# One 512-column stream per weight load in the late down products of a two-mixture kernel

## The chip, the core and the metric

The program runs on one core of one Trainium2 chip, alone. Its time is device time in microseconds, the median of several executions of one program. Three executions of the kernel before took 929.62, 928.58 and 929.4 us; the median is 929.4.

## The reference, cut to what matters

The reference is a kernelized attention whose output goes through two dense mixtures, one after the other. The change touches only the last product of each, `... @ w_out`, called the down product here.

```
x = attention(q, k, v, omega)                 # 2304 tokens x 512
g = x @ w_gate; val = x @ w_val               # 512 -> 1536
x = (g * sigmoid(g) * val) @ w_out            # 1536 -> 512, first down product
h = x @ w_in                                  # 512 -> 2048
g = where(h >= 1, h, where(h <= -1, 0, (h + 1)**2 / 4))
out = g @ w_out                               # 2048 -> 512, second down product
```

## The kernel before

**Three matmuls for one product.** Every 32-bit factor is kept as two tiles of the type fp32r, a high part and a low rest. `split3` (L418 to L420) multiplies them with three matmuls: high by high, high by low, low by high. Each matmul loads a stationary block of 128 by 128 into TensorE (LDWEIGHTS, shown as PEld) and streams the moving operand through it.

**Stages.** Attention and the first mixture's early steps share the time up to about 225 us. The rest of the first mixture and all of the second form the late part: four passes, two for each mixture, over five blocks of tokens (four of 512 tokens, the last of 256). In a pass `late_up` makes the up products of each block: seven products of 256 columns built from sums and differences of quarters (`set_up`), so that one product is saved. ScalarE (ACT) and VectorE (DVE) turn them into activations and split these into rows `hl` or `hlr` (`row_out`). `late_down` then multiplies each row by its part of `w_out` and adds it up in four banks of PSUM, `acc[0]` to `acc[3]`, a whole pass long.

**The down products.** In the first mixture (`down1`) the stationary block is a 128-column piece of the weight and the tokens stream. In the second (`down2`, and `down_end` for the last two rows) the stationary block is a 128-token piece of the row and the weight's 512 columns stream. In a name such as `bank<-hl,w` the moving tile comes first: `bank<-hl,w` is a product of the first mixture, `bank<-w,hl` one of the second. Both stream 256 columns at a time and go over the same stationary blocks twice, once for each half of the bank.

**What orders the work.** No engine order is written out by hand. `Planner` simulates the engines with a cost for each operation and records an instruction when its simulated engine comes to it. PE takes the operation of the lowest rank first: up products have 2.0, down products 2.1, so a down product is placed when its row is ready by the plan and no up product is. DVE and ACT go by rank too: the preparation of the weights (`stage`: from the two words of a 64-bit number to 32 bits, lines L435 to L442, stored in DRAM as `w32`) comes last at 1.5, and `w_feed` fetches the weights of the next pass back as soon as slots are free. `copy` (L399 on ACT, L401 on DVE) goes to whichever of the two would be done sooner by the plan. PE's cost is `c_pe`. On the chip each engine runs its list in order and waits on semaphores.

Of the kernel before, what the change touches and what calls it, by code (L numbers as in the profile page):

```python
# [28 lines left out]
P = 128  # L29
TB = 256  # L30
# [255 lines left out]


def c_pe(n):
    return max(0.109, n * 0.1134 / 256)


@with_exitstack
def performer_moe_kernel(ctx: ExitStack, tc: tile.TileContext, qX, kX, vX, om, ident,
# [17 lines left out]
    acc = []  # L311
# [105 lines left out]
    def split3(ps, l_hi, l_lo, r_hi, r_lo, first, last, shared=False):  # L417
        nc.tensor.matmul(ps, l_hi, r_hi, start=first, stop=False, skip_group_check=shared)  # L418
        nc.tensor.matmul(ps, l_hi, r_lo, start=False, stop=False, skip_group_check=shared)  # L419
        nc.tensor.matmul(ps, l_lo, r_hi, start=False, stop=last, skip_group_check=shared)  # L420
# [570 lines left out]
    def evac_late(a, kb, n):  # L991
        nt = blocks[kb][1]
        rng = (osb, xin)[n % 2]
        xb = yield Get(rng)
        yield x2_part_ready[a, kb, n]
        pb = x2_part.pop((a, kb, n))
        x, part, ac = xb[:, 0:nt], pb[:, 0:nt], acc[n][:, 0:nt]
        if n % 2:
            yield Op("ACT", c_act(nt), lambda: nc.scalar.activation(x, ac, AF.Copy, scale=0.5))
            pl.set(acc_free[n])  # L1000
            yield from two(x, x, part, nt, ALU.add)
        else:
            yield Op("DVE", c_dve(nt), lambda: nc.vector.scalar_tensor_tensor(
                out=x, in0=ac, scalar=0.5, in1=part, op0=ALU.mult, op1=ALU.add))
            pl.set(acc_free[n])
        pl.put(xpart, pb)
        pl.cur.rank = 1.0
        if a < len(SETS1) - 1:
            yield from dma(x2q[a][kb][:, n, 0:nt], x, P * nt * 4)
            pl.set(x2p_ready[a + 1, kb, n])  # L1010
        else:
            yield from dma(x2d[n // 2][:, n % 2, kb * 512:kb * 512 + nt], x, P * nt * 4)
        pl.put(rng, xb)
        if a == len(SETS1) - 1:
            x2_cnt[kb] = x2_cnt.get(kb, 0) + 1
            if x2_cnt[kb] == KD:
                pl.set(x2_ready[kb])
# [24 lines left out]
    def out1(step, h_ev, res):  # L1042
        k, fp = step
        first, last, end = run[step]
        for i in range(2):
            yield wready["o", 2 * fp + i]
        yield h_ev
        ws = [wslot["o", 2 * fp + i] for i in range(2)]
        hl = res[0]
        for n in range(KD):  # L1050
            d, c = divmod(n, 2)
            if first and c == 0:
                acc1[d] = yield Get(bank, -2)
            for i in range(2):
                yield Op("PE", 3 * c_pe(TB), lambda: split3(
                    acc1[d][:, c * TB:(c + 1) * TB], ws[i][:, 0, n * P:(n + 1) * P], ws[i][:, 1, n * P:(n + 1) * P],
                    hl[:, 0, i * TB:(i + 1) * TB], hl[:, 1, i * TB:(i + 1) * TB],
                    first and c == 0 and i == 0, last and i == 1, True), kind="moe")
            if last and c == 1:
                pl.spawn(evac1(k, d, end, acc1[d]))  # L1060
        pl.put(hrow, res[1])
        for f in (2 * fp, 2 * fp + 1):
            if last_use[f] == step:
                wfree(("o", f), wring)

    def moe1():
        pend = None
        for step in steps1:
# [12 lines left out]
            for s in ("g", "v"):  # L1081
                yield wready[s, 2 * fp]
                ps = yield Get(bank, -1)
                for i in range(2):
                    f = 2 * fp + i
                    yield wready[s, f]
                    w = wslot[s, f]
                    yield Op("PE", 12 * c_pe(TB), lambda: gemm(ps[:, i * TB:(i + 1) * TB], w), kind="moe")
                    if last_use[f] == step:
                        wfree((s, f), wring)  # L1090
                if s == "g":
                    pl.spawn(elem1(ps, vps, v_ev, (h_ev, res)))
                else:
                    vps.append(ps)
                    pl.set(v_ev)
# [119 lines left out]
    half2 = [slice(0, 256), slice(256, 512)]  # L1215
    rows = {}
    before = got = None
    for m, a, order, sets in passes:
        for j in order:
            for c in sets:  # L1220
                n = 2 if m == 1 and j < 4 else 1 if m == 1 else 4 if j < 4 else 2
# [213 lines left out]
    def evac2(a, j, c):  # L1435
        t0, nt = blocks[j]
        x = yield Get(osb)
        end = a == len(SETS2) - 1
        ro = out[t0 + c * P:t0 + (c + 1) * P, :] if end else opart[a, j, c]
        if a == 0:  # L1440
            yield from copy(x, acc[c], 512, False)
            pl.set(acc_free[c])
            yield from dma(ro, x, 262144)
        else:
            yield part2_ready[a - 1, j, c]
            pb = part2.pop((a - 1, j, c))
            yield Op("DVE", c_dve(512), lambda: nc.vector.tensor_tensor(out=x, in0=acc[c], in1=pb, op=ALU.add))
            pl.set(acc_free[c])
            pl.put(xpart, pb)
            yield from dma(ro, x, 262144)  # L1450
        if not end:
            pl.set(opart_ready[a, j, c])
        pl.put(osb, x)
# [11 lines left out]
    def down1(a, j, f, hl, cols, first, last):  # L1465

        nt = blocks[j][1]
        yield wready["o", f]
        w = wslot["o", f]
        for n in range(KD):  # L1470
            if first:
                while len(acc) <= n:
                    acc.append((yield Get(bank, -2)))
                yield acc_free[n]
                acc_free[n] = Ev()


            def prod():
                for t in range(0, nt, TB):
                    h = slice(cols.start + t, cols.start + t + TB)  # L1480
                    split3(acc[n][:, t:t + TB], w[:, 0, n * P:(n + 1) * P], w[:, 1, n * P:(n + 1) * P],
                           hl[:, 0, h], hl[:, 1, h], first and t == 0, last, True)
            yield Op("PE", 3 * c_pe(nt), prod)
            if last:
                pl.spawn(evac_late(a, j, n))

    def down2(a, j, f, hl, cols, first, last):
        nt = blocks[j][1]
        yield wready["p", f]
        w = wslot["p", f]  # L1490
        for c in range(nt // P):
            if first:
                yield acc_free[c]
                acc_free[c] = Ev()
            h = slice(cols.start + c * P, cols.start + (c + 1) * P)


            def prod():
                for d in half2:
                    split3(acc[c][:, d], hl[:, 0, h], hl[:, 1, h], w[:, 0, d], w[:, 1, d], first and d.start == 0, last, True)  # L1500
            yield Op("PE", 3 * c_pe(512), prod)
            if last:
                pl.spawn(evac2(a, j, c))

    def evac_end(a, j, c, done):
        t0 = blocks[j][0]
        x = yield Get(osb)
        yield part2_ready[a - 1, j, c]
        pb = part2.pop((a - 1, j, c))
        for h, ev in zip(half2, done):  # L1510
            yield ev
            yield Op("DVE", c_dve(256), lambda: nc.vector.tensor_tensor(out=x[:, h], in0=acc[c][:, h], in1=pb[:, h], op=ALU.add))
            last = pl.spawn(dma(out[t0 + c * P:t0 + (c + 1) * P, h], x[:, h], P * 1024))
        yield last

    def down_end(a, j, pair, hl):
        ws = []
        for f, _ in pair:
            yield wready["p", f]
            ws.append(wslot["p", f])  # L1520
        for c in range(2):
            hs = [slice(cols.start + c * P, cols.start + (c + 1) * P) for _, cols in pair]
            for i in range(2 - c):
                def prod(i=i, c=c):
                    for d in half2:
                        split3(acc[c][:, d], hl[:, 0, hs[i]], hl[:, 1, hs[i]], ws[i][:, 0, d], ws[i][:, 1, d], False, i + c == 1, True)
                yield Op("PE", 3 * c_pe(512), prod)
            if c == 0:
                pl.spawn(evac2(a, j, c))
        done = [Ev(), Ev()]  # L1530
        pl.spawn(evac_end(a, j, 1, done))
        for h, ev in zip(half2, done):
            yield Op("PE", 3 * c_pe(TB), lambda: split3(
                acc[1][:, h], hl[:, 0, hs[1]], hl[:, 1, hs[1]], ws[1][:, 0, h], ws[1][:, 1, h], False, True, True))
            pl.set(ev)
# [140 lines left out]
```

## Time and profile before

| what | value |
|---|---|
| median of the timed runs | 929.4 us |
| the profiled execution's span, first to last instruction | 928.9 us |
| PE, matmuls | 920.5 us, 99%, 9244 instructions |
| PEld, weight loads | 905.8 us, 98%, 9244 instructions |
| DVE | 775.1 us, 83%, 1496 instructions |
| ACT | 511.7 us, 55%, 1131 instructions |
| 16 DMA engines, main queue | 48.5% of their time |

The profile shows one execution. Its own time outside the span isn't shown; the median is 0.5 us above the span. A matmul's recorded duration reaches from its start to its last result, so that durations overlap: what one costs TensorE is the distance from start to start.

### The profile page before, as it was taken

How to read it: one execution, taken by the hardware profiler on the slowest of the kernel's cores; microseconds unless marked ns; L12 is line 12 of the kernel's file. 1: busy time of each engine (PE TensorE's matmuls, PEld its weight loads, DVE VectorE, ACT ScalarE, POOL GpSimd, SP SyncE). 2: the span in 40 equal slices, each digit the busy share in tenths (PEclk: the TensorE clock that was granted, in tenths of full speed). 3: DMA queues.
4: the chain of work that ended last, by engine and by line, in shares of the span. 5: the costliest groups of instructions: out<-in, count | busy, mean ns of one | idle time of the engine just before them, and what ended most of it. 6: DMA issues, size and time to landing. Idle time of an engine off the chain costs nothing.

```text
span 928.9 us, 22669 instructions
## 1 busy us (share of the span) xinstructions
PE 920.5 (99%) x9244; PEld 905.8 (98%) x9244; DVE 775.1 (83%) x1496; ACT 511.7 (55%) x1131; POOL 61.7 (7%) x53
## 2 busy tenths in 40 slices
PE   9999999999999999999999999999999999999998
PEld 7899999999999999999999999999999999999998
DVE  5999888766989998999989999999797669767553
ACT  7888877544445545554545556554555445444331
POOL 0222314222000000000000000000000000000000
PEclk9999999999999999999999999999999999999999
DMA  7578356555665374946476836264313131403022
GB/s 242 193 246 280 111 178 214 191 182 178 221 233 179 114 245 167 303 131 197 142 231 218 271 110 200 80 225 139 126 58 125 47 102 47 137 12 103 9 84 91
DMA packets 88665, 147.71 MB, mean 159 GB/s; under 512 B 8304, under 2 KB 43888, under 8 KB 88560
## 3 DMA queue, kind: packets, MB, share of 16 engines
q1 hardware_dynamic: 88560, 146.26, 48.5%
q8 instruction: 72, 1.18, 0.5%
q14 instruction: 33, 0.27, 0.1%
HBM read 103.24 MB, written 42.99 MB: 157 GB/s over the span
## 4 chain that ended last, share of the span: by engine, by line
PE 88%; DVE 5%; DMA 4%; ACT 1%; issue 1%; SPq 0%; DVEq 0%; ACTq 0%
PE bank L418 26%; PE bank L420 25%; PE bank L419 25%; PE bank L654 5%; PE bank L723 2%; PE bank L836 2%; PE bank L792 2%; PE bank L846 1%; DMA wtr<-w32i 1%; DMA ws<-in_w_dram 1%; DMA ws<-in_wo_dram 1%; DMA x2d<-os 1%; DMA xr<-x2p 1%; DMA xq<-x1d 1%; DMA kl<-in_kX_dram 1%
## 5 line engine op out<-in xcount | busy, mean ns | idle before, releaser
L418 PE MATMUL bank<-x1s,w 128*128 128x256 f32 x492 | 138.2, 281 | 0.5 <-ACT eb L399 0.3
L419 PE MATMUL bank<-x1s,w 128*128 128x256 f32 x492 | 136.4, 277 | 0.0
L420 PE MATMUL bank<-x1s,w 128*128 128x256 f32 x492 | 136.4, 277 | 0.0
L418 PEld LDWEIGHTS bank<-x1s,w 128*128 128x128 f32 x492 | 92.5, 188 | 1.6 <-ACT eb L399 0.5
L419 PEld LDWEIGHTS bank<-x1s,w 128*128 128x128 f32 x492 | 92.5, 188 | 0.0
L420 PEld LDWEIGHTS bank<-x1s,w 128*128 128x128 f32 x492 | 92.5, 188 | 0.0
L399 ACT ACTIVATE x1s<-xq 128x512 fp32r<-128x512 f32 x84 | 52.7, 629 | 59.1 <-PE bank L420 34.7
L418 PE MATMUL bank<-x1s,wb 128*128 128x256 f32 x286 | 78.9, 276 | 0.0
L419 PE MATMUL bank<-x1s,wb 128*128 128x256 f32 x286 | 78.9, 276 | 0.0
L420 PE MATMUL bank<-x1s,wb 128*128 128x256 f32 x286 | 78.9, 276 | 0.0
L418 PE MATMUL bank<-x1s,wx 128*128 128x256 f32 x278 | 77.3, 278 | 0.7 <-ACT eb L399 0.7
L419 PE MATMUL bank<-x1s,wx 128*128 128x256 f32 x278 | 76.8, 276 | 0.0
L420 PE MATMUL bank<-x1s,wx 128*128 128x256 f32 x278 | 76.8, 276 | 0.0
L435 ACT ACTIVATE wt<-ws 128x512 f32<-128x512 f32 x68 | 46.0, 678 | 45.2 <-DMA ws<-in_w_dram 24.4
L399 ACT ACTIVATE eb<-bank 128x512 f32<-128x512 f32 x96 | 56.5, 589 | 25.2 <-PE bank L420 24.7
L411 DVE TENSOR_TENSOR x1s<-xq,x1s 128x512 fp32r<-128x512 f32 x90 | 61.7, 686 | 8.0 <-ACT x1s L399 7.8
L663 DVE TENSOR_REDUCE st<-bank 128x4 f32<-128x512 f32 (+1 forms) x76 | 47.9, 657 | 17.8 <-PE bank L654 17.7
L1248 DVE TENSOR_TENSOR gb<-bank,eb 128x512 f32<-128x512 f32 x64 | 43.9, 686 | 12.9 <-PE bank L420 12.7
L399 ACT ACTIVATE hlr<-hb 128x512 fp32r<-128x512 f32 x54 | 34.0, 630 | 36.1 <-PE bank L419 21.9
L418 PEld LDWEIGHTS bank<-x1s,wb 128*128 128x128 f32 x286 | 53.7, 188 | 0.0
L419 PEld LDWEIGHTS bank<-x1s,wb 128*128 128x128 f32 x286 | 53.7, 188 | 0.0
L420 PEld LDWEIGHTS bank<-x1s,wb 128*128 128x128 f32 x286 | 53.7, 188 | 0.0
(253 smaller groups left out, 3328.6 us busy)
## 6 DMA issues: line engine op xcount, KB each, us to landing
ws<-in_w_dram SPq DMA_DIRECT2D x40, 512.0 KB, 4.9
ws<-in_wo_dram SPq DMA_DIRECT2D x28, 512.0 KB, 5.4
xq<-x1d SPq DMA_DIRECT2D x36, 256.0 KB, 4.5
xq<-x2d SPq DMA_DIRECT2D x36, 256.0 KB, 4.2
qi<-in_qX_dram SPq DMA_DIRECT2D x28, 256.0 KB, 4.0
ki<-in_kX_dram SPq DMA_DIRECT2D x22, 256.0 KB, 4.4
x1d<-os SPq DMA_DIRECT2D x18, 256.0 KB, 4.3
op<-os SPq DMA_DIRECT2D x18, 256.0 KB, 2.7
```

The costliest lines, as they stand in the source:

```text
L399: yield Op("ACT", c_act(n), lambda: nc.scalar.activation(dst, src, AF.Copy, scale=1.0 if scale is None else scale))
L411: yield Op("DVE", c_dve(n), lambda: nc.vector.tensor_tensor(out=dst, in0=a, in1=b, op=op), True)
L418: nc.tensor.matmul(ps, l_hi, r_hi, start=first, stop=False, skip_group_check=shared)
L419: nc.tensor.matmul(ps, l_hi, r_lo, start=False, stop=False, skip_group_check=shared)
L420: nc.tensor.matmul(ps, l_lo, r_hi, start=False, stop=last, skip_group_check=shared)
L435: yield Op("ACT", 0.575, lambda: nc.scalar.activation(t, hw.bitcast(F32), AF.Abs))
L654: nc.tensor.matmul(banks[a][:, u * P:(u + 1) * P], xb[h, l, u * P:(u + 1) * P], r[h], start=first and (last or u == 0), stop=last, skip_gr ...
L663: yield Op("DVE", c_dve(256 * n), lambda: nc.vector.tensor_reduce(out=sv[:, a, units, 3 if by_pe else 0], in_=pv[a], axis=AX.X, op=ALU.max ...
L723: nc.tensor.matmul(kp[h, 2 * pr + a, 0:65], es[:, a, u * P + 64 * m:u * P + 64 * m + 64], v[:, 65 * a:65 * a + 65], start=(li == 0 and a = ...
L792: nc.tensor.transpose(tp[:, (a * 2 + t) * P:(a * 2 + t + 1) * P], es[:, a, u * P:(u + 1) * P], ids)
L836: nc.tensor.matmul(banks[t][rows, 65 * h:65 * h + 65], q_t[:, h // 2, h % 2, t * P + 64 * m:t * P + 64 * m + 64], kvr[tiles[t][m], d][:, h ...
L1248: yield Op("DVE", c_dve(512), lambda: nc.vector.tensor_tensor(out=dst, in0=pq(ps), in1=pq(e), op=ALU.add))
```

## The change

The two halves of each late down product become one: the same three matmuls of `split3`, each on 512 columns. This holds for the four blocks of 512 tokens in the first mixture and for all of the second, except the last two half products of the program. The up products, the early down products (`out1`) and the first mixture's block of 256 tokens stay at 256 columns. The planner's cost of a matmul is changed too: at 256 columns it stays 0.1134 us, at 512 columns it falls from 0.2268 to 0.2168 us, and at 128 columns it rises from 0.109 to 0.1134.

```
 def c_pe(n):
-    return max(0.109, n * 0.1134 / 256)
+    return max(0.1134, n / 2400.0 + 0.0035)
...
             def prod():
-                for t in range(0, nt, TB):
-                    h = slice(cols.start + t, cols.start + t + TB)
-                    split3(acc[n][:, t:t + TB], w[:, 0, n * P:(n + 1) * P], w[:, 1, n * P:(n + 1) * P],
-                           hl[:, 0, h], hl[:, 1, h], first and t == 0, last, True)
+                h = slice(cols.start, cols.start + nt)
+                split3(acc[n][:, 0:nt], w[:, 0, n * P:(n + 1) * P], w[:, 1, n * P:(n + 1) * P],
+                       hl[:, 0, h], hl[:, 1, h], first, last, True)
             yield Op("PE", 3 * c_pe(nt), prod)
...
             def prod():
-                for d in half2:
-                    split3(acc[c][:, d], hl[:, 0, h], hl[:, 1, h], w[:, 0, d], w[:, 1, d], first and d.start == 0, last, True)
+                split3(acc[c], hl[:, 0, h], hl[:, 1, h], w[:, 0], w[:, 1], first, last, True)
             yield Op("PE", 3 * c_pe(512), prod)
...
                 def prod(i=i, c=c):
-                    for d in half2:
-                        split3(acc[c][:, d], hl[:, 0, hs[i]], hl[:, 1, hs[i]], ws[i][:, 0, d], ws[i][:, 1, d], False, i + c == 1, True)
+                    split3(acc[c], hl[:, 0, hs[i]], hl[:, 1, hs[i]], ws[i][:, 0], ws[i][:, 1], False, i + c == 1, True)
                 yield Op("PE", 3 * c_pe(512), prod)
```

In the program 2490 matmuls of 256 columns become 1245 of 512, with 1245 weight loads fewer. On PE, at the first late down product between two up products (`x1s_72` by a weight; `hlr` by the weight `wb_3550` is the down product):

```order
 L419 MATMUL bank_70<-x1s_72,w_111 128x256
 L420 MATMUL bank_70<-x1s_72,w_111 128x256
-L418 MATMUL bank_65<-hlr,wb_3550 128x256
-L419 MATMUL bank_65<-hlr,wb_3550 128x256
-L420 MATMUL bank_65<-hlr,wb_3550 128x256
-L418 MATMUL bank_65<-hlr,wb_3550 128x256
-L419 MATMUL bank_65<-hlr,wb_3550 128x256
-L420 MATMUL bank_65<-hlr,wb_3550 128x256
+L418 MATMUL bank_65<-hlr,wb_3550 128x512
+L419 MATMUL bank_65<-hlr,wb_3550 128x512
+L420 MATMUL bank_65<-hlr,wb_3550 128x512
 L418 MATMUL bank_70<-x1s_72,w_117 128x256
```

Six rows became three, at the same place; the neighbours stay.

Further on in the first mixture, PE's list is ordered anew. Before, a down product (`hl` by `wb_3551`) stands right between two products of the up part:

```order
L418 MATMUL bank_67<-x1s_73,w_113 128x256
L419 MATMUL bank_67<-x1s_73,w_113 128x256
L420 MATMUL bank_67<-x1s_73,w_113 128x256
L418 MATMUL bank_65<-hl,wb_3551 128x256
L419 MATMUL bank_65<-hl,wb_3551 128x256
L420 MATMUL bank_65<-hl,wb_3551 128x256
```

With the change the same up product is followed by further up products:

```order
L418 MATMUL bank_67<-x1s_73,w_113 128x256
L419 MATMUL bank_67<-x1s_73,w_113 128x256
L420 MATMUL bank_67<-x1s_73,w_113 128x256
L418 MATMUL bank_70<-x1s_72,wx_957 128x256
L419 MATMUL bank_70<-x1s_72,wx_957 128x256
L420 MATMUL bank_70<-x1s_72,wx_957 128x256
```

Thirty rows of up products now stand ahead of this down product, where none stood before. The interleaving of up and down products is ordered anew in this way between some 390 and 535 us of the trace before; ahead of it and behind it the two orders agree but for one or two places.

On DVE, in the first mixture's late part (`wt` and `ws` are tiles of the weight preparation, L436 to L442; `os` is an accumulator on its way to DRAM, `eb` the copy of a product's bank):

```order
 L411 TENSOR_TENSOR xq_3540<-xq_3537,xq_3540 128x512
-L411 TENSOR_TENSOR hlr<-hb_100,hlr 128x512
-L436 TENSOR_SCALAR wt_78<-wt_78 128x512
-L438 TENSOR_SCALAR wt_78<-wt_78 128x512
-L440 SCALAR_TENSOR_TENSOR wt_78<-ws_76,wt_78 128x512
-L442 SCALAR_TENSOR_TENSOR wt_78<-ws_76,wt_78 128x512
+L401 COPY eb_3529<-bank_69 128x512
+L436 TENSOR_SCALAR wt_78<-wt_78 128x512
 L1003 SCALAR_TENSOR_TENSOR os_103<-bank_65,xr_3526 128x512
```

A bank's copy moved from ACT to DVE, and three steps of the weight preparation moved back behind the accumulator. Over the program seven copies more are on DVE and seven fewer on ACT: 1500 rows on DVE where there were 1493, 869 on ACT where there were 876. SP issues the same number of transfers, those of the weight preparation later among the others.

## Rows read from the trace of the kernel before

**Rows 1.** The page: busy time of engines; PE's share and granted clock by slices.
```profile
PE 920.5 (99%) x9244; PEld 905.8 (98%) x9244; DVE 775.1 (83%) x1496; ACT 511.7 (55%) x1131; POOL 61.7 (7%) x53
...
PE   9999999999999999999999999999999999999998
...
PEclk9999999999999999999999999999999999999999
```

**Rows 2.** Windows: us; busy us (instructions) of PE, PEld, DVE, ACT, POOL; PEclk; DMA.
```profile
225.00:500.00 275.00, 273.64 (x2400) 272.50 (x2399) 256.50 (x486) 142.58 (x262) 1.29 (x1) 1.00 0.61 200
500.00:720.00 220.00, 220.00 (x1942) 219.95 (x1941) 202.40 (x377) 122.44 (x226) 0.00 (x0) 1.00 0.46 149
720.00:929.00 209.00, 204.62 (x1806) 204.42 (x1804) 135.89 (x235) 82.00 (x146) 0.00 (x0) 1.00 0.22 70
425.00:450.00 25.00, 25.00 (x222) 24.95 (x221) 24.83 (x51) 15.05 (x29) 0.00 (x0) 1.00 0.68 222
525.00:575.00 50.00, 50.00 (x444) 50.00 (x443) 50.00 (x94) 31.47 (x59) 0.00 (x0) 1.00 0.56 178
625.00:675.00 50.00, 50.00 (x443) 50.00 (x442) 42.03 (x76) 25.67 (x46) 0.00 (x0) 1.00 0.42 136
```

**Rows 3.** Timeline of PE, 860 to 880 us: start, duration, instruction.
```profile
859.74 0.28 PE L420 MATMUL bank<-wx,hlr 128*128 128x256 f32 x1
859.86 0.28 PE L418 MATMUL bank<-x1s,wx 128*128 128x256 f32 x1
...
879.92 0.28 PE L418 MATMUL bank<-w,hlr 128*128 128x256 f32 x1
```

**Rows 4.** The chain that ended last, 408 to 475 us and behind: start, us, what.
```profile
408.39 0.13 PE bank L420
...
414.14 5.20 DMA xq<-x1d
...
424.33 0.60 DVE gb L1248
...
474.85 0.50 ACT eb L399
475.39 0.38 PE bank L418
```

**Rows 5.** PE's matmuls on `hl`, by windows: us, busy (instructions), clock, DMA.
```profile
408.00:475.00 67.00, 14.14 (x96) 1.00 0.62 195
475.00:929.00 454.00, 137.00 (x1008) 1.00 0.36 117
625.00:929.00 304.00, 99.68 (x748) 1.00 0.26 85
```

**Rows 6.** The same of the matmuls on `hlr`.
```profile
408.00:475.00 67.00, 16.33 (x113) 1.00 0.62 195
475.00:929.00 454.00, 137.48 (x1008) 1.00 0.36 117
625.00:929.00 304.00, 99.75 (x744) 1.00 0.26 85
```

**Rows 7.** Groups by line: weight loads by shape, copies on DVE; busy us, mean ns.
```profile
L418 PEld LDWEIGHTS bank<-hlr,w 128*128 128x128 f32 x80 | 15.0, 188 | 0.0
...
L723 PEld LDWEIGHTS bank<-vi,ebk 128*64 128x64 f32 x640 | 20.2, 137 | 2.2 <-issue 0.3
...
L792 PEld LDWEIGHTS bank<-ids,ebq 128*128 128x128 f32 x144 | 15.7, 141 | 2.0 <-ACT ebq L684 0.8
...
L401 DVE COPY os<-bank 128x512 f32<-128x512 f32 x6 | 4.1, 688 | 2.5 <-PE bank L420 1.5 <-PE bank L846 0.6 <-DMA ki<-in_kX_dram 0.5
...
L401 DVE CAST hlr<-hb 128x512 fp32r<-128x512 f32 x3 | 1.3, 420 | 0.0
```

**Rows 8.** The chain that ended last, eight transposes (128 columns each) on end.
```profile
111.43 0.87 PE bank L792 x8
```

**Rows 9.** Timeline of PE, 162 to 165 us, in the first mixture's early part.
```profile
162.65 0.28 PE L418 MATMUL bank<-hl,w 128*128 128x256 f32 x1
...
164.88 0.28 PE L419 MATMUL bank<-x1s,w 128*128 128x256 f32 x1
```

**Rows 10.** Weight preparation: its last step by tile; the later fetch, from SP's timeline.
```profile
L442 DVE SCALAR_TENSOR_TENSOR wt<-ws,wt x14: 680/684/694, 506.5 to 656.0; 128x512 uint32<-128x512 uint32 x14
...
698.57 0.38 SPq L392 DMA_DIRECT2D wtr<-w32p x1
```

## The prediction

> **What bounds the kernel now.** I read the page's busy shares first. PE and its weight loads are busy 99% and 98% of the span, DVE 83%, and the granted clock is full in all forty slices, so TensorE runs at its upper level, 2.4 GHz [rows 1]. A busy share of PE says little by itself, since a matmul's record reaches to its last result; so the second view is the timeline of PE, where the starts tell what one matmul takes from the next. From 859.74 to 879.92 us there are 179 starts in a row, up and down products mixed, so 178 steps in 20.18 us: 113.4 ns each (113.37) [rows 3]. At 2.4 GHz 256 columns need 106.7 ns; 6.7 ns of each step are something else. The third view is the chain that ended last. It runs through PE alone from 475 us on but for moments, to the tail at 924 us; before that it leaves PE at 408.39 us and goes through DVE, ACT and a transfer to a matmul that starts at 475.39 us behind a copy on ACT [rows 4]. The fourth view, windows, says the same of the engines: PE lacks 1.4 us of 275 from 225 to 500 us, nothing from 500 to 720 us, and 4.4 of the last 209 us, which is the program's tail behind the last matmul [rows 2]. DVE is the engine to watch: 24.83 of 25 us at 425 us, 50.00 of 50 from 525 to 575 us, but 42 of 50 behind 625 us and 65% behind 720 us [rows 2]. So PE sets the time nearly everywhere, with DVE close behind it up to about 625 us.
>
> **The change, part by part.** It removes 1245 matmuls and as many weight loads, and moves the same columns. What it brings is therefore the difference between two steps of 256 columns and one of 512, 1245 times. Two steps take 2 x 113.37 = 226.7 ns, whatever the neighbour [rows 3].
>
> No row shows a 512-column step of this type at full clock, so I bound it. It can't be shorter than the stream itself, 512 columns at 2.4 GHz, 213.3 ns, which would bring 13.4 ns a pair, 16.7 us in all. If the step grew with the columns it would be 226.7 ns, and nothing would be gained. In between, if the 6.7 ns are paid by each matmul whatever its length, it is 220.0 ns, and the gain is 6.7 x 1245 = 8.3 us.
>
> Which of these? Look at what the 6.7 ns could be. A weight load of 128 columns is recorded with 188 ns, one of 64 columns with 137 [rows 7]: 51 ns for 64 columns, so about 102 ns for 128, nearly as long as the stream of 256 columns above which it has to hide. And eight transposes, each 128 moved columns with a block of 128 columns loaded (141 ns in the records, shorter than the 188), take 0.87 us, 109 ns each [rows 7, 8]: with half the columns of a product the step falls by only 4 ns. So at 256 columns and below something like the weight load, not the stream, sets the step. Under 512 columns the load has more than 100 ns to spare. What is left is the small rest that the transposes show, 109 against 106.7, some 2.3 ns, if it is paid there for the same reason. I take 216 ns, near the lower end: 226.7 - 216 = 10.7 ns a pair, 1245 x 10.7 = 13.3 us. The caveat is that transposes are of another type (f32, not fp32r), so their step may be made up of something else.
>
> The Trainium skill's page "TensorE: Matmul & The Clock Gate", section "Back-to-back issue gap", gives N/2.4 + 2.5 ns for the gap of a warm matmul: 215.8 ns at 512 columns, and a gain of (226.7 - 215.8) x 1245 = 13.6 us, an estimate from that page. At 256 columns it would give 109.2 ns, and here the trace differs: 113.4 [rows 3]. If what the formula lacks, 4.2 ns, belongs to every matmul, it speaks against my price, with 220 ns and 8.3 us.
>
> Where is the gain on the path? The windows count the late down products by the tile that they read. From 475 us to the end there are 1008 on `hl` and 1008 on `hlr` [rows 5, 6]; less some 54 that stay at 256 columns (the second pass's block of 256 tokens, the last two halves), about 980 pairs. These stand in a stretch in which PE waits for nothing, and their 10.5 us come off the end in full as long as the other engines follow. From 408 to 475 us, 209 matmuls, at most 104 pairs, stand beside a chain that isn't PE's [rows 4 to 6]: there a faster PE only waits longer for the same DVE work, so I count their 1.1 us as lost, 1.0 rounded. The rest, some 160 pairs ahead of 408 us, lies on PE's chain.
>
> The moves. The planner's order changes between about 390 and 535 us: up products run ahead of down products, for PE would otherwise be early for rows that DVE hasn't made. That costs PE nothing while there are up products to do and rows and banks are free; I cost it at nothing, with the idle time there as it is. If that cover is gone, a wait costs what the last one on the chain costs, some tenths of a us. Seven copies go from ACT to DVE: two copies of a bank at 688 ns, the other five casts at 420 [rows 7], 3.5 us of DVE by their records in the whole program. Outside the saturated stretches they lie beside PE's work and cost nothing; inside they are at most those 3.5 us. The weight preparation moves back on DVE and its transfers on SP. Its last step is at 656 us and the fetches of the next pass's weights still go on at 698 us [rows 10], so there are some 40 us in hand and I cost the move at nothing; without that, PE would wait at the start of the last pass for a weight. The accumulators are read once a pass as before, the tail is unchanged, and no wait is added inside a down product.
>
> The sum, on the profiled execution: 928.9 - 13.3 + 1.0 = 916.6 us of span. The median of the runs is 0.5 above that span; I keep this, and predict 917.1 us.
>
> **The rivals.** First, *the 6.7 ns belong to each matmul*: the step is 220 ns and the gain 8.3 us, less 0.7 lost to DVE between 408 and 475 us: 921.8. For it: products of 256 columns have the same step whether they share a stationary block with a neighbour or not. In the early part a step is even 117.4 ns: 19 steps from 162.65 to 164.88 us [rows 9], so something about the tiles can add 4 ns to a step there; if the same were to hit a 512-column stream, it would be as dear as this rival. Against it: the transposes' 109 ns.
>
> Second, *DVE becomes the bound*. It has the same work, and 3.5 us more, in less time; where it is full, PE's gain turns into waits. If all ahead of 475 us is lost, 980 x 10.7 = 10.5 us stay, 918.9. If everything up to 625 us is lost, there remain (748 + 744 - 6) / 2 = 743 pairs [rows 5, 6], 8.0 us: 921.4. Against it: from 500 to 720 us PE has no idle time although DVE is at 92% there [rows 2], and part of DVE's load is weight preparation that can wait.
>
> Third, *the step grows with the columns*: no gain, 929.4. A stream bound by something other than the clock would do this. The transposes speak against it: half the columns take 96% of the time.
>
> Fourth, *slower*: the new order between 390 and 535 us makes PE wait. Its place is an up product that needs a bank which DVE or ACT hasn't emptied, since their work stands behind a row whose slot is held by a down product placed thirty rows later. The wait at 475 us is of this kind. PE lacks 1.4 us in the 275 us ahead of 500 us [rows 2]; such waits would have to grow by the whole 13.3 us, ten times as much, before the time is no better, and by over 15 us to be slower beyond doubt. If they grew by 18 us, the kernel would take 934. The order of the plan shows more up products ahead, not fewer, so little speaks for it.
>
> **How the numbers follow.** The forecast (step of 215 to 217.5 ns, up to 2 us lost to DVE) has 0.52; the fixed cost for each matmul 0.20; DVE as the bound 0.18; no gain 0.05; slower 0.05. The likeliest gives 917.1. Its own range is 914 to 919.5: below, a step of 215 ns (14.6 us) with nothing lost; above, one of 217.5 ns (11.5 us) with 2 us lost. The range that should hold 8 times in 10 adds the fixed cost and DVE as the bound, both near 922, and 1 us more of waits: 914.0 to 923.0. Leaving out 0.2% (about 1.9 us) as what a measurement can't tell from no change: faster 0.92, the same 0.04, slower 0.04.
>
> **What would show it.** In the trace after, late down products of 512 columns: starts 216 ns apart inside one `split3`, and 1245 PE and PEld rows fewer (7999). 220 ns would show the fixed cost, 226.7 the third rival. Up products should still stand 113.4 ns apart, the one behind a down product too. The windows behind 500 us should show PE without idle time, and the chain PE alone from some 475 us on. DVE as the bound would show as a chain that leaves PE between 400 and 625 us for much longer than the 67 us of now, and as PE's idle time there. I am wrong if the 512-column step is above 221 ns, or if PE's idle time between 225 and 720 us grows by over 5 us.

## The result, and the profile after

The changed kernel takes 936.3 us (median of four runs, 935.98 to 936.62) where the kernel before takes 929.5: a ratio of 1.0065 with a 95% interval of 1.0048 to 1.0082. It is slower by 7 us; forecast were 917.1.

The profiled execution of the changed kernel took 936.07 us and its span is 934.3, so 1.8 us lie around it. The span grew by 5.4 us over that of before (928.9). In every run that lists both, time and span lie 1.8 us apart, so the execution of before that was profiled took about 930.7 us, 1.3 above its median; the 0.5 us between median and span that the prediction kept came of this, and so does it that the spans grow by less than the medians. The page's busy times, and its slices for PE and the weight loads:

```profile
PE 927.6 (99%) x7999; PEld 861.7 (92%) x7999; DVE 778.0 (83%) x1503; ACT 507.9 (54%) x1124; POOL 62.5 (7%) x53
...
PE   9999999999999999999999999999999999999998
PEld 7899999999999999999999999999998889999986
```

The change did what it says: 7999 matmuls and loads where [rows 1] has 9244, 1245 fewer, and the loads' busy share falls from 98% to 92%. PE is as busy as before. The windows, with PE's and DVE's busy time as second and fourth figure:

```profile
225.00:500.00 275.00, 274.82 (x2089) 261.66 (x2088) 254.77 (x484) 141.61 (x262) 1.56 (x2) 1.00 0.60 195
500.00:720.00 220.00, 220.00 (x1513) 203.15 (x1512) 204.44 (x381) 118.50 (x219) 0.00 (x0) 1.00 0.47 155
720.00:929.00 209.00, 209.00 (x1293) 187.15 (x1292) 138.69 (x240) 82.86 (x148) 0.00 (x0) 1.00 0.21 67
```

Against [rows 2], PE waits less, not more: it lacks 0.2 us of the 275 from 225 us on, where it lacked 1.4. The last window is full only because the last matmul starts later, at 930.44 us where it was 924.34. DVE isn't late anywhere that PE shows. So the time isn't in waits; it is in the matmuls. The timeline of PE around one merged down product of the second mixture, start and recorded duration:

```profile
640.23 0.28 PE L419 MATMUL bank<-x1s,wb 128*128 128x256 f32 x1
640.35 0.28 PE L420 MATMUL bank<-x1s,wb 128*128 128x256 f32 x1
640.46 0.39 PE L418 MATMUL bank<-w,hlr 128*128 128x512 f32 x1
640.69 0.39 PE L419 MATMUL bank<-w,hlr 128*128 128x512 f32 x1
640.91 0.39 PE L420 MATMUL bank<-w,hlr 128*128 128x512 f32 x1
641.15 0.28 PE L418 MATMUL bank<-x1s,wb 128*128 128x256 f32 x1
641.27 0.28 PE L419 MATMUL bank<-x1s,wb 128*128 128x256 f32 x1
641.39 0.28 PE L420 MATMUL bank<-x1s,wb 128*128 128x256 f32 x1
641.50 0.28 PE L418 MATMUL bank<-x1s,wb 128*128 128x256 f32 x1
```

The three starts of 512 columns stand 0.23, 0.22 and 0.24 us from the next one, and the two steps behind them take 0.12 where the steps of [rows 3] take 0.113. Over all 216 merged products of the second mixture that stand before an up product, the averages, from the starts in the trace, are 226.0, 229.0 and 233.3 ns for the three matmuls, and 121.7 and 116.0 ns for the two behind. Together that is 688.3 ns where six matmuls of 256 columns take 680, and 11.0 ns more on these two neighbours than at 113.3: 19.3 ns lost per merged product.

### The profile page after: what moved, and what is told of

It reads as the page before. It is cut to its first block, busy times and chain, and to the rows that moved or that the text cites. A ratio compares the mean times of both kernels' runs of the same rounds, so it can differ in the third digit from the quotient of the medians.

```text
span 934.3 us, 20172 instructions
## 1 busy us (share of the span) xinstructions
PE 927.6 (99%) x7999; PEld 861.7 (92%) x7999; DVE 778.0 (83%) x1503; ACT 507.9 (54%) x1124; POOL 62.5 (7%) x53
## 4 chain that ended last, share of the span: by engine, by line
PE 95%; DMA 3%; ACT 1%; DVE 1%; SPq 0%; issue 0%; DVEq 0%
PE bank L418 28%; PE bank L419 28%; PE bank L420 28%; PE bank L654 5%; PE bank L723 2%; PE bank L836 2%; PE bank L792 2%; PE bank L846 1%; DMA wtr<-w32g 1%; DMA wty<-w32o 1%; DMA ws<-in_w_dram 1%; DMA ids<-in_ident_dram 0%; SPq L392 0%; ACT ebq L676 0%; DMA w32v<-wt 0%; DVE st L663 0%
## 5 line engine op out<-in xcount | busy, mean ns | idle before, releaser
L1248 DVE TENSOR_TENSOR gb<-bank,eb 128x512 f32<-128x512 f32 x64 | 44.0, 688 | 17.7 <-PE bank L420 17.3
L419 PEld LDWEIGHTS bank<-x1s,wb 128*128 128x128 f32 x286 | 53.6, 187 | 4.3
L418 PEld LDWEIGHTS bank<-x1s,wb 128*128 128x128 f32 x286 | 53.8, 188 | 4.0
L418 PEld LDWEIGHTS bank<-x1s,wx 128*128 128x128 f32 x278 | 52.3, 188 | 3.5
L419 PEld LDWEIGHTS bank<-x1s,wx 128*128 128x128 f32 x278 | 52.1, 188 | 3.7
```

## The experiments

The theory after the result (A): a step of 256 columns was never held up by a cost of each matmul that a longer stream would hide. The step of this type goes with its columns. That the place of the stream and the weight block in SBUF matters was no part of A at first; it came in with e4, as A1 against A2 (the place doesn't matter). The rivals: the planner's new order costs the time (O); a 512-column step alone takes 216 to 220 ns (B), or does so on an idle core and is disturbed in the kernel (C).

**e1_steps_alone: the steps by themselves.** On an otherwise idle core, runs of sixty matmuls:

```
for a in run(20, 512):        # 20 products of three; also 128, 192, 256, 320, 384, 448
    nc.tensor.matmul(a[0], a[1], a[2], start=a[3], stop=a[4])
    ...
for a in run(20, 512, wh, mh):  # the same in bf16, also 256
    ...
```

> Leaves the whole computation out: it loads two pieces of q, makes high and low tiles of them, and issues on an otherwise idle core runs of sixty matmuls of 128, 192, 256, 320, 384, 448 and 512 columns (fp32r, three to a product as in the kernel, each with its weight load), then ten times one product of 512 columns followed by four of 256, then runs of bf16 at 256 and 512. Theory A (the stream's own pace: 256 columns take 113.3 ns because the stream does, not the load): steps grow in proportion, 226 to 230 ns at 512, 170 at 384, and at 128 the load sets about 107 to 109. Theory B (my prediction's: a load or a fixed cost sets the step at 256): 216 to 220 ns at 512, 160 to 167 at 384. Theory C (216 alone, 229 only in the kernel, for DVE, ACT and DMA disturb the longer stream): 216 here. In the pattern, A says that the products of 256 columns behind one of 512 lose some ns here too, as in the changed kernel (121.7 and 116.0 ns).

The list of one line's matmuls (count; duration min, median, max; first and last start; shape) of the runs at 256 and 512 columns, fp32r and then bf16:

```profile
L61 PE MATMUL bank<-mv,wt x60: 280/283/302, 35.5 to 42.6; 128*128 128x256 f32 x60
L69 PE MATMUL bank<-mv,wt x60: 387/389/398, 74.3 to 87.7; 128*128 128x512 f32 x60
L73 PE MATMUL bank<-mh,wh x60: 272/273/283, 109.2 to 115.7; 128*128 128x256 bf16 x60
```

From first to last there are 59 steps: (42.6 - 35.5) / 59 = 120 ns at 256 columns, (87.7 - 74.3) / 59 = 227 at 512, and 110 for bf16 at 256. From the single starts, away from the ends of a run:

```
columns, fp32r   128    192    256    320    384    448    512   | bf16 256   512
step, ns       111.6  111.7  120.0  146.7  173.3  206.7  226.7   |    109.2  215.8
```

B and C fall: on an idle core 512 columns of fp32r take 226.7 ns. The 216 ns that I had put into the sum exist, but in bf16. The Trainium skill's page "TensorE: Matmul & The Clock Gate", section "Back-to-back issue gap", gives N/2.4 + 2.5 ns for what it calls the isolated gap of a matmul; both bf16 steps here agree with it, back to back and each with its load. For fp32r from 256 columns on the formula is too short, by 11 to 18 ns in this run.

At 128 and at 192 columns the step is the same, 111.6 ns, near the 109 ns of the transposes of [rows 8]; at 256 columns it is longer. One thing I hadn't expected: 256 columns took 120.0 ns here, not 113.3. So this run doesn't show steps in proportion to the columns, as A had it: twice 120.0 would be 240. At 256, 320, 384 and 512 columns the step is 13.3 ns above the columns' time at 2.4 GHz, at 448 it is 20.0 above; taken alone, this looks much like a fixed cost of each matmul, of twice the size that the prediction's first rival gave it.

The run also held ten times one product of 512 columns followed by four of 256. A expected the products behind to lose some ns here too, and they didn't: the first matmul behind took 116 or 117 ns in nine of the ten, less than 120.0, while the three steps of 512 columns took 232 to 234, 235 to 237 and 227 to 229.

**e2_merge_old_order and e3_order_old_matmuls: the two halves of the change.** Two kernels split the change into its matmuls and its order.

```
 def c_pe(n):                      # e2: the changed kernel with the old cost
-    return max(0.1134, n / 2400.0 + 0.0035)
+    return max(0.109, n * 0.1134 / 256)
 def c_pe(n):                      # e3: the kernel before with the new cost
-    return max(0.109, n * 0.1134 / 256)
+    return max(0.1134, n / 2400.0 + 0.0035)
```

> The 512-column matmuls with the old planner cost, so that every engine's order is that of the kernel before. Theory A (the matmuls themselves cost it): 415 products of 512 columns cost some 19 ns more each than twice 256, neighbours included, 8 us: 936 to 938 us, ratio to before about 1.008. Theory O (the new order costs it): 929 us or better, ratio 1.000 or below.

> The old 256-column matmuls in the order of the changed kernel: only the planner's cost is changed. Theory A: PE's idle time between 296 and 572 us falls by some 2 us as in the changed kernel, so 926.5 to 929 us, ratio 0.997 to 1.000. Theory O (the new order costs it): 934 to 937 us, ratio 1.006.

e2, the matmuls without the new order, took 940.2 us: ratio 1.0113, interval 1.0094 to 1.0132. e3, the order without the matmuls, took 927.4: ratio 0.9974, interval 0.9964 to 0.9984. The windows from 225 to 500 us of e2, and then of e3:

```profile
225.00:500.00 275.00, 273.39 (x2076) 260.06 (x2075) 255.38 (x489) 142.13 (x261) 2.57 (x2) 1.00 0.61 198
```

```profile
225.00:500.00 275.00, 275.00 (x2419) 274.68 (x2418) 256.37 (x487) 142.83 (x265) 1.47 (x2) 1.00 0.61 198
```

With the old order PE lacks 1.6 us here, with the new one nothing. Theory O falls: the order is the good half of the change. Against the runs of before that stand beside them (median 929.7 us), the order alone brings 2.3 us and the merge alone costs 10.5; with the new order the merge costs 8.9 (936.3 - 927.4). e2 is dearer than I expected (936 to 938). Idle time doesn't explain that, since PE lacks nearly as much in the kernel before, 1.4 us; its six runs lie between 937.5 and 942.8, and the profiled one has a span 8.5 us above that of before, close to the 8 us expected. e3 beats both kernels.

**e4_place_sweep: the place.** The 120.0 of e1 against 113.3 in the kernel asked for this one: the moving operand is shifted in steps of 32 bytes, the block stays.

```
for b in range(0, 256, 8):                      # floats: 32 bytes
    for x in same(0, b, 512, 16):               # block at 0, stream at b
        nc.tensor.matmul(x[0], x[1], x[2], start=x[3], stop=x[4])
```

> Leaves the whole computation out: runs of fp32r matmuls on an otherwise idle core, the moving operand's place in SBUF shifted in steps of 32 bytes against the stationary block's; first one block and one stream of 512 columns over and over, then the same at 256, then products of three matmuls at 512 and at 256. Theory A1 (the surcharge comes from the weight load and the stream meeting in SBUF, so the place decides): the step varies with the shift in units of 6.7 ns, 113 to 120 at 256 columns and 220 to 233 at 512, with some shifts at 220 or below. Theory A2 (the fp32r stream has its pace, whatever the place): 226 to 227 at 512 for nearly every shift, no shift below 225.

Mean steps from the starts in the trace; each column holds four shifts, 256 bytes apart, which agree within 0.6 ns:

```
shift, bytes (mod 256)    0     32     64     96    128    160    192    224
512 columns, ns       226.7  233.5  229.2  233.1  233.3  234.2  233.3  233.1
256 columns, ns       119.8  117.8  117.8  119.2  118.7  117.3  113.3  117.8
```

A1 holds in that the step changes with the shift; my guess of shifts at 220 ns or below was wrong, none is below 226.6. The pattern repeats every 256 bytes. In the third part of this run, with products of three, the block was moved too, by 128 and by 192 bytes, and the places of 226.7 ns moved with it: it is the place of the stream against the block that counts. It isn't all that counts: of the 24 pairs of runs of products at 256 columns that lie 256 bytes apart two differ, the one by 4 ns (113.3 and 117.8). What else decides there wasn't tested.

At 192 bytes 256 columns take 113.3 ns, which is the step of the kernel before, and it is their best place; 512 columns take 233.3 there, nearly their worst. So what comes on top of the columns' time at 2.4 GHz is no fixed cost: at this place it is 6.7 ns for 256 columns and 20.0 for 512, at shift 0 some 13 for both. And the best 512-column step, 226.7, is twice the best 256-column step. Nothing in this sweep lets the merge gain on a kernel whose 256-column steps all stand at 113.3.

**e5_mix_places: the kernel's mix.** Six up matmuls of 256 columns and one down product, in both forms, at 64 placements.

> Leaves the whole computation out: on an otherwise idle core, the kernel's own mix, six up matmuls of 256 columns and one down product, six times on end, for 64 placements in SBUF (the up part's moving tile, the row and the down weight each shifted by 0, 64, 128 or 192 bytes against the up weight), first with the down product as three matmuls of 512 columns, then as six of 256. Theory A1 (each load meets the streams beside it, the place decides): one repeat takes 1360 to 1440 ns in either form; the placements that give the six 256-column matmuls 113.3 ns each (1360 a repeat) are not those at which 512 columns take 226.7; the best of the merged form is 1360 or a little above, not below. If some placement of the merged form falls to 1340 or below, the merge could win with other padding, and my reading that it can't is wrong.

At one of them the kernel is seen again, step for step. The timeline of two repeats with the merged product (`x,up` is the up part, `wo,row` the down product), the moving tile of the up part shifted by 192 bytes, the row by 128, the down weight by 192:

```profile
521.42 0.85 PE L57 MATMUL bank<-x,up 128*128 128x256 f32 x6
522.11 0.85 PE L57 MATMUL bank<-wo,row 128*128 128x512 f32 x3
522.80 0.85 PE L57 MATMUL bank<-x,up 128*128 128x256 f32 x6
```

The same placement with the split product:

```profile
1063.70 0.84 PE L62 MATMUL bank<-x,up 128*128 128x256 f32 x6
1064.38 0.84 PE L62 MATMUL bank<-wo,row 128*128 128x256 f32 x6
1065.06 0.84 PE L62 MATMUL bank<-x,up 128*128 128x256 f32 x6
```

A repeat takes 1.38 us merged and 1.36 split: 20 ns more, as the 19.3 in the kernel. The merged steps are 226, 229 and 234 ns for the product and 121, 116, 114, 114, 113, 113 for the six behind it, the series of the changed kernel. So an idle core is enough for the loss on the two matmuls behind; why it falls on these two isn't shown. Over the 64 placements the merged form takes 1380 to 1420 ns a repeat on average (single repeats come down to 1366) and the split form 1360 to 1440. The merged one is faster at 54 of them; but 1360 stands at three placements of the split form and at none of the merged.

**e6_split_rows_moved and e7_merge_rows_moved: the place in the kernel.** One number moves the rows of the second mixture by 192 bytes in SBUF, from offset 48 to 0 in floats; no instruction changes its place in any list.

```
-O_OFF, P_OFF, H_OFF = 32, 48, 48
+O_OFF, P_OFF, H_OFF = 32, 48, 0
```

> The kernel before with the rows of the second mixture moved by 192 bytes in SBUF (H_OFF from 48 to 0), the order of every engine the same. If the place of stream and block against each other decides the step (theory A1): the mix measured alone goes from 1360 to 1426 ns a repeat at this shift, 66 ns for each of 217 down products that stand between up products, 14 us, and more for the 70 that stand among themselves: 940 to 950 us, ratio 1.012 to 1.022. If places don't matter in the kernel (A2): 929.5 us, ratio 1.000.

> The changed kernel with the same shift of the rows. A1: the merged form stays at 1380 ns a repeat in the mix measured alone, so 933 to 938 us, and at this placement the merge wins, by 5 to 14 us against the run with the split form. A2: 936 us, the merge loses by 7 us as at the old place.

The kernel before with this shift took 947.6 us, ratio 1.0187 (1.0158 to 1.0217); the changed kernel with it 935.7, ratio 1.0063 (1.0046 to 1.0080). The timeline of one split down product in e6:

```profile
640.96 0.28 PE L418 MATMUL bank<-w,hlr 128*128 128x256 f32 x1
641.08 0.28 PE L419 MATMUL bank<-w,hlr 128*128 128x256 f32 x1
641.20 0.28 PE L420 MATMUL bank<-w,hlr 128*128 128x256 f32 x1
641.32 0.28 PE L418 MATMUL bank<-w,hlr 128*128 128x256 f32 x1
641.44 0.28 PE L419 MATMUL bank<-w,hlr 128*128 128x256 f32 x1
641.56 0.28 PE L420 MATMUL bank<-w,hlr 128*128 128x256 f32 x1
641.68 0.28 PE L418 MATMUL bank<-x1s,wb 128*128 128x256 f32 x1
```

Six steps of 120 ns, with the same tiles, shapes and order that took 113.3 before. The up products, none of whose tiles moved, get slower too: from 572 us on a step averages 118.2 ns on them and 119.7 on the down products, where both took 113.3. Over 1378 and 1715 matmuls that is 17.7 us, the 18 us of the whole run. One merged down product in e7:

```profile
640.34 0.40 PE L418 MATMUL bank<-w,hlr 128*128 128x512 f32 x1
640.57 0.40 PE L419 MATMUL bank<-w,hlr 128*128 128x512 f32 x1
640.80 0.39 PE L420 MATMUL bank<-w,hlr 128*128 128x512 f32 x1
641.04 0.28 PE L418 MATMUL bank<-x1s,wb 128*128 128x256 f32 x1
641.15 0.28 PE L419 MATMUL bank<-x1s,wb 128*128 128x256 f32 x1
```

Here the long steps average 231.7 ns from 572 us on (229.3 in the changed kernel) and the up products 113.4 (115.1): the loss has moved from the neighbours to the merged product itself, and the sum stays. In e5 the matching shift, the row at 192 bytes where it lay at 128 (64 up is 192 down in a pattern of 256), makes a repeat 1426 ns split and 1380 merged. At this placement the merge gains 11.9 us (947.6 - 935.7); at the old one it loses 6.8, the new order's 2.3 us included in both. A1 stands, with both signs of the merge shown.

## Why the prediction was wrong

**What bounds the kernel** was right: PE sets the time, the clock is full, and with the order's help PE waits less, not more. DVE didn't become the bound, so the 1.0 us counted as lost to it wasn't lost in this way; e3 shows the new order as a gain of 2.3 us, which I had costed at nothing.

**The step that failed** is the price of the 512-column step. I took 216 ns, because "at 256 columns and below something like the weight load, not the stream, sets the step". Measured are 226.0, 229.0 and 233.3 in the kernel (229.5 over all 1245: 88.30 us for 384 in the first mixture, 197.43 for 861 in the second), well over the 221 ns that I had named as the sign of being wrong. The transposes did show a floor near 110 ns at 128 columns, and e1 shows it for fp32r too (111.6), so the type, my caveat, wasn't what misled. What misled was to carry the floor up to 256 columns, since 113.3 happens to lie close to it: e1 has 120.0 there, and from 256 columns on each step is longer than the one before. The 2.3 ns that I let a 512-column step keep had no ground either: they compared the transposes' 109 ns with the 106.7 of a 256-column stream, two different things. The runs show 13.3 to 20.9 ns above the stream's 213.3 instead, by place.

**The upper bound was no bound.** I wrote that the step "would be 226.7 ns" if it grew with the columns, and took that as the most; no gain was the worst that I gave the merge itself. But 113.3, the step of the kernel before, is the best of eight places in e4, and a 512-column stream at that place takes 233.3. A bound from the rows of one form held for that form's placement only.

**The neighbours** were taken to keep their 113.4 ns. The two behind a merged product take 121.7 and 116.0. Of the change's loss these neighbours are the larger half: 11.0 of 19.3 ns.

**The sum again**, with what was measured. 344 merged products stand before an up product: 344 x 19.3 = 6.6 us. The other 71, all but one of them before another down product of 512 columns, take 226 + 229 + 231.7 = 686.7 ns, 6.7 more than before: 0.5 us. PE's idle time goes down by 2.2 us between 296 and 572 us. That makes 4.9 of the 6.1 us by which the last matmul starts later (930.44 after, 924.34 before). Of the remaining 1.2 us, some 0.7 are up products of 117 ns or so between 350 and 450 us that aren't among the three behind a merged product; I haven't tested what makes them longer. The rest isn't located.

**The rivals.** The one of no gain (the step grows with the columns) was nearest to the time, and at the best places, 113.3 and 226.7 ns, to the steps. The fixed cost of each matmul fails as I priced it, since no 512-column step of fp32r averages below 226.6 ns in e1 or e4; that it is no fixed cost of another size either is shown by e4, not by e1. The slower rival named the wrong place: it looked for waits in the new order. Its sign was right, and that is luck. The early-part steps of 117.4 ns [rows 9] were the trace's only hint of what happened: the same shape took 4 ns more, and I noted that "something about the tiles can add 4 ns", and gave it to a rival that still ended faster.

## What to carry to other kernels

Fewer weight loads under a longer stream gain only where the long step, with its neighbours, is shorter than the short steps that it replaces; measure both, in the type and at the places used, before counting on it. Where stream and block lie against each other in SBUF can be worth 6% of a 256-column step and 3% of a 512-column one, and a layout tuned for one shape of matmul has to be tuned anew for another: in e5 the placement that looks like the old layout gives the split form 1360 ns a repeat and the merged one 1380, and the shifted one 1426 and 1380. The part of this change worth keeping is the planner's cost alone (e3, 927.4 us).

## What the runs showed of the hardware

A TensorE step of fp32r depends on the place of the moving operand against the stationary block, with a period of 256 bytes but for two runs of e4: 113.3 to 119.8 ns at 256 columns, 226.7 to 234.2 at 512. The best place for 256 columns is nearly the worst for 512. The Trainium skill's page "TensorE: Matmul & The Clock Gate", section "Step-by-step: what each phase is for", says that loading the next block doesn't take SBUF read bandwidth from the running matmul, by two ports of their own; these runs neither confirm nor refute that. What they show is that moving the stream by 32 bytes, or the block by 128 or 192, changes the step on an idle core, and that moving only the down products' blocks slows the up products beside them (e6). That load and stream meet in the memory is my reading of it; no run here showed the memory itself, and a stream without any load wasn't tried. Nor is it shown why even the best places take 6.7 ns above the bare 106.7 of 256 columns, where bf16 takes 2.5.
